# Weight loads on ScalarE's DMA queue, and attention slots moved to the first feed-forward half

## The chip, the core and the metric

The kernel runs on one core of a Trainium2 chip. A core has a matrix engine (TensorE, PE in the profile; its weight loads are PEld), a vector engine (VectorE, DVE), a scalar engine (ScalarE, ACT), a general engine (GpSimd, POOL) and a sync engine (SyncE, SP) that here only issues DMAs. Each engine works through its own list of instructions in order. DMAs are issued by SP and by ACT, each on a queue of its own (q1 and q10 in the profile); a DMA instruction that waits for something holds up whatever stands behind it on the engine that issues it. The metric is the device time of one execution in microseconds; less is better.

## The reference

```python
batch, n_heads, seq, head_dim = (8, 8, 576, 64)
n_tokens, d_model, d_ff = (4608, 512, 2048)

def _attn_ref(q, k, v, s):
    scores = scale * np.matmul(q, k.transpose(0, 1, 3, 2))
    cum = np.cumsum(np.maximum(s, 0.0), axis=-1)
    bias = -(cum[:, :, :, None] - cum[:, :, None, :])
    scores = np.where(causal, -1000000000.0, scores + np.minimum(bias, 0.0))
    scores = scores - np.max(scores, axis=-1, keepdims=True)
    attn = np.exp(scores)
    attn = attn / (np.sum(attn, axis=-1, keepdims=True) + 1e-09)
    return np.matmul(attn, v)

def _moe_ref(x, w_in, w_out):
    h = x @ w_in
    g = np.where(h >= 1, h, np.where(h <= -1, 0.0, (h + 1) ** 2 / 4))
    return g @ w_out
```

The output of the attention, with its heads side by side, is the input `x` of the feed-forward layer. The two weight matrices arrive as 64-bit numbers.

## The kernel before

**Attention.** Heads are taken in pairs, 32 pairs `n` for 8 batches of 4. A batch's 576 query rows are cut in two halves `hf`, of 320 and 256 columns. One pair in one half is a job: 64 jobs, for each batch four of the first half and then four of the second. A job is cut into 8 slots (`att_slot(j, k)`): slot 0 prepares Q and K, slots 2 to 7 each compute one block of scores, slot 3 also loads the next job's Q and K, and slot 7 also issues `att_out` of the job before. For a block of scores PE multiplies Q by K into a PSUM tile `s` (L405 for the first eight jobs, L410 and L411 later; there are two such tiles, shared with `px`), DVE adds the mask and finds the minimum `mn` (L416), ACT takes the exponential (L427), DVE gets the reciprocal of the sum `rs` (L443, L444), POOL, ACT and DVE write the scaled weights as two half-precision parts `pb` (L448 to L451, L454), and SP issues a DMA transpose of `pb` into `pt` (L455). `att_out` multiplies `pt` with `vt`, the transposed V, into `px` (L473), and ACT and DVE write it to `X[b, hf]` (L484 for the first half of all, L490 and L491 later). Names such as `p3_4_1` are pair 3, query tile 4, head 1.

**Weights.** Each matrix comes in 16 chunks of 512 KB (`Weights`, `w1` for `w_in`, `w2` for `w_out`). `load` (L190) brings a chunk into a raw buffer `wir` or `wor`; `decode` makes 32-bit floats of it: ACT L199, DVE L200, a matmul of the sums for a bound (L204), and then either ACT L212 and DVE L213 or DVE L215 and L216. The last of these frees the raw buffer for a later chunk. `w1` has four raw buffers; `w2` has two of one kind and two that it shares with tiles of `X`. `scale` takes the bound of a group of chunks (L220 to L223), and `split` makes two half-precision parts, with ACT L229 and L231 and POOL L232. The chunk's place in `WT` gives the name: `WT2` to `WT17` are the chunks of `w1` and `WT18` to `WT33` those of `w2` as they are decoded. The first three loads of `w2` wait for the bound of the last group of `w1`, by a small copy (L185).

**Feed-forward.** Its 16 halves run one after the other. The first half of all uses 32-bit matmuls (`first_h`, L566, needs `X[0, 0]` of the first four jobs and the decoded `w1`; `first_y`, L584, needs the decoded `w2`). All later halves use the split parts: `ffn_h` (L534) takes 16 tiles `h` one after the other, ACT, DVE and POOL make `g` of each, and `ffn_y` (L611) adds it into four tiles `y`, two steps behind.

**Order.** The program is written as loops: first four jobs with the 16 chunks of `w1`, then 512 steps `j`. In each step stand one attention slot, or two, then parts of the weights' work, then feed-forward work; step 32 opens the second half. A scheduler then sets the order of each engine's instructions: the written order is their priority, some parts have a higher one (`tc.high_priority`), and an instruction is taken when the scheduler believes that it can run. The order on the engines so differs from the written one.

Of the kernel before, what the change touches and what calls it, by code (L numbers as in the profile page):

```python
# [25 lines left out]
NFT = DFF // P  # L26
# [43 lines left out]
@with_exitstack  # L70
def attention_ffn(ctx: ExitStack, tc: tile.TileContext, qT, kT, vT, s, w_in, w_out, yT):
    nc = tc.nc
    LOADQ, CUMQ = nc.sync, nc.scalar
    V, A, G, T = nc.vector, nc.scalar, nc.gpsimd, nc.tensor

    cp = ctx.enter_context(tc.tile_pool(name="cp", bufs=1))
# [91 lines left out]
    class Weights:  # L168
# [10 lines left out]
        def load(self, n, after=None):  # L179
            if n < NW:  # L180
                c = self.order[n]
                pool, tag, bufs = self.tags[n % len(self.tags)]
                self.raw[c] = pool.tile([P, NC, 2], I32, tag=tag, bufs=bufs, name=f"{self.name}r{c}")
                if after is not None:
                    V.tensor_copy(self.raw[c][:, 0, :1], after.bitcast(I32))  # L185
                src = self.src(c)
                dst = self.raw[c]
                if len(src.shape) == 4:
                    dst = dst.rearrange("p (j n) t -> p j n t", j=2)
                nc.sync.dma_start(dst, src)  # L190

        def decode(self, n):
            c, g = self.order[n], n // self.size
# [79 lines left out]
    def batch_scales(b):  # L273
        m = msc[b]
        h = hsc[b] = ap.tile([P, 4], F32, tag="hs", name=f"hs{b}")
        V.tensor_scalar(h, w1.bound, m, 2.0 ** -27, ALU.mult, ALU.mult)

        r = rsc[b] = ap.tile([P, 1], F32, tag="r", name=f"r{b}")
        i = r.bitcast(I32)
        V.tensor_scalar(r, m, a_in, 4.0, ALU.mult, ALU.mult)  # L280
        V.tensor_scalar(r, r, 1.0, None, ALU.max)
        V.reciprocal(r, r)
        V.tensor_scalar(r, r, 2.0 ** 14, None, ALU.mult)
        V.tensor_scalar(i, i, 23, None, ALU.logical_shift_right)
        V.tensor_scalar(i, i, 127, None, ALU.add)
        V.tensor_scalar(i, i, 1, 23, ALU.logical_shift_right, ALU.logical_shift_left)

        u = usc[b] = ap.tile([P, 4], F32, tag="us", name=f"us{b}")
        V.tensor_scalar(u, h, r, None, ALU.mult)
        w = wsc[b] = ap.tile([P, 4], F32, tag="ws", name=f"ws{b}")  # L290
        V.tensor_scalar(w, u, 2.0, None, ALU.mult)
        c = ubi[b] = ap.tile([P, 1], F32, tag="ub", name=f"ub{b}")
        V.tensor_scalar(c, r, 0.5, None, ALU.mult)
        g = gsc[b] = ap.tile([P, 1], F32, tag="gb", name=f"gb{b}")
        V.reciprocal(g, r)
        V.tensor_scalar(g, g, g, 2.0 ** 14, ALU.mult, ALU.mult)

    def batch_y(b, groups=(0, 1)):
        ysc.setdefault(b, {})
        for i in groups:  # L300
            y = ysc[b][i] = ap.tile([P, 1], F32, tag=f"ys{i}", name=f"ys{b}_{i}")
            V.tensor_scalar(y, gsc[b], w2.bound[:, i:i + 1], 2.0 ** -28, ALU.mult, ALU.mult)
# [197 lines left out]
    def att_slot(j, k):  # L500

        if j < len(jobs):
            n, hf = jobs[j]
            if k == 0:
                att_prep(n, hf)
            if k == 1 and hf == 0:
                v_prep(n)
            if k == V_K and hf == 0:
                v_turn(n)
            if k >= 2:  # L510
                scores(n, *UNITS[hf][k - 2])
            if k == 3 and j + 1 < len(jobs):
                att_load(*jobs[j + 1])
            if k == 1 and j % (2 * NPAIR) == V_J and j // (2 * NPAIR) + 1 < B:
                load_v(j // (2 * NPAIR) + 1)
            if k == 5 and j + 1 < len(jobs) and jobs[j + 1][0] % NPAIR == 0 and jobs[j + 1][1] == 0:
                with tc.issue_after(ttr[0]):
                    batch_start(jobs[j + 1][0] // NPAIR)
        if k == OUT_K and 1 <= j <= len(jobs) and j != NPAIR:
            while j == len(jobs) and late:  # L520
                late.pop(0)()
            att_out(*jobs[j - 1])
# [39 lines left out]
    def first_h(ft):  # L562
        N = HALF[0][1]
        h = ps_h.tile([P, 512], F32, tag="h", name=f"h0_0_{ft}")
        for kt in range(NKT):
            T.matmul(  # L566
                h[:, :N], flat32(w1.held[ft // 4 * NKT + kt])[:, ft % 4 * P:(ft % 4 + 1) * P], X[0, 0][:, kt],
                start=(kt == 0), stop=(kt == NKT - 1),
            )
        if ft % 4 == 0:  # L570
            g32.append(gp.tile([P, 4, N], F32, tag="g", bufs=G_BUFS, name=f"g0_0_{ft}"))
        with tc.high_priority(offset=FFN_LEAD):
            u = gp.tile([P, N], F32, tag="u", bufs=4, name=f"u0_0_{ft}")
            A.activation(u, h[:, :N], AF.Relu, bias=half_bias, scale=us32)
            V.scalar_tensor_tensor(h[:, :N], h[:, :N], ws32, u, ALU.mult, ALU.max)
            V.scalar_tensor_tensor(g32[-1][:, ft % 4], u, 1.0, h[:, :N], ALU.min, ALU.mult)

    def first_y(ft, ms):
        N = HALF[0][1]
        for m in ms:  # L580
            if ft == 0:
                ys[0, 0, m] = ps_y.tile([P, 512], F32, tag=f"y{m}", name=f"y0_0_{m}")
            c0 = ft % 2 * 2 * P + m % 2 * P
            T.matmul(  # L584
                ys[0, 0, m][:, :N], flat32(w2.held[8 * (m // 2) + ft // 2])[:, c0:c0 + P], g32[ft // 4][:, ft % 4],
                start=(ft == 0), stop=(ft == NFT - 1),
            )
            if ft == NFT - 1:
                o = gp.tile([P, N], F32, tag="o", bufs=O_BUFS, name=f"o0_0_{m}")
                with tc.high_priority(offset=FFN_LEAD):  # L590
                    A.copy(o, ys[0, 0, m][:, :N])
                nc.scalar.dma_start(yT[m * P:(m + 1) * P, :N], o)
# [37 lines left out]
    def ffn_step(s, k):  # L630

        b, hf, ft = s // (2 * NFT), s // NFT % 2, s % NFT
        if k == 0:
            ffn_q.append((b, hf, ft, ffn_h(b, hf, ft)))
        elif len(ffn_q) > Y_LAG:
            ffn_y(*ffn_q.pop(0))
# [26 lines left out]
    for j in range(16 * NP):  # L663
        if j % 64 == 48 and j // 64 + 1 < B:
            batch_scales(j // 64 + 1)
            batch_y(j // 64 + 1)

        for _ in range(1 + (j % 4 == 3 if j < 2 * NFT else j % 8 == 3 and j < 6 * NFT)):
            att_slot(t // 8, t % 8)
            t += 1  # L670
        if j < NW // 2:
            with tc.high_priority(offset=W2_LEAD):
                for c in (2 * j, 2 * j + 1):
                    w2.decode(c)
                    w2.load(c + 3)
                    if c % 8 == 7:
                        w2.scale(c // 8, TINY)
        if j < NFT:
            first_h(j)
        elif j < 2 * NFT:  # L680
            i = j - NFT
            if i < 8:
                for ft in (2 * i, 2 * i + 1):
                    first_y(ft, (0, 1))
            else:
                for ft in range(i % 4 * 4, i % 4 * 4 + 4):
                    first_y(ft, (i // 4,))
        if j == NFT:
            V.tensor_reduce(a_in, w1.bound, axis=AX, op=ALU.max)
            batch_scales(0)  # L690
            batch_y(0)
        if 4 <= j < NW + 4:
            w1.split(j - 4)
        if NW + 8 <= j < 2 * NW:
            w2.split(j - NW - 8)
        elif 2 * NW <= j < 2 * NW + 4:
            with tc.high_priority(offset=W2_LEAD):
                for c in (8, 9):
                    w2.split(c + (j - 2 * NW) * 2)
        if j >= 2 * NFT:  # L700
            ffn_step(j // 2, j % 2)
# [32 lines left out]
```

## Time and profile before

| | |
|---|---|
| median of 3 runs | 1121.34 us (1119.88 to 1121.64) |
| the profiled execution | 1119.59 us, of which the span is 1117.8 |
| busy in the span | PE 1024.0 us, DVE 836.8, ACT 731.0, POOL 667.6 |
| granted TensorE clock, mean | 0.98 |
| DMA queues | q1 (SP) 143.49 MB, 60.3% of 16 engines' time; q10 (ACT) 9.93 MB, 2.9% |
| weight loads | 32 of 512 KB, issued from 1.4 to 142.6 us |

In a row of a timeline stand the start in us, the duration, the engine and the line, the operation with its output and input, how often it is repeated, and in brackets the idle time ahead of it and what ended that. "SPq" and "ACTq" are DMA issues; the transfer itself ends later. In a row of stretches the columns are named where it is shown. In the groups of the page stand the summed busy time, the mean of one in ns, and the idle time ahead.

### The profile page before, as it was taken

To read this page: it belongs to the slowest core of one execution; us is meant where nothing else is said; L and a number is where in the kernel's file an instruction comes from. 1 tells how busy PE (TensorE), PEld (TensorE's weight loads), DVE (VectorE), ACT (ScalarE), POOL (GpSimd) and SP (SyncE) were. 2 spreads that over 40 slices of the span, in tenths; PEclk is the share of its full clock that TensorE was granted. 3 is DMA by queue.
4 is the path that set the end of the run, shared out by engine and by line. 5 is a ranking of instruction groups with operands and counts; after the bars stand their busy time and mean duration, and the time that the engine had idled before them with its cause. 6 is when DMAs were issued, how large, how long until landed. Compare 5 with 4: busy or idle time off the path is not lost.

```text
span 1117.8 us, 24800 instructions
## 1 busy us (share of the span) xinstructions
PE 1024.0 (92%) x8366; PEld 787.3 (70%) x8368; DVE 836.8 (75%) x2313; ACT 731.0 (65%) x1703; POOL 667.6 (60%) x1163
## 2 busy tenths in 40 slices
PE   2668897699999999999999999899999999899998
PEld 1335565487777877777778877777778877787787
DVE  7865775778778877878778878777787877887533
ACT  4656669667557774767557774767577765777432
POOL 4642558776557654766557755666557664765522
PEclk9999899699998999999999999999999999999999
DMA  7995633687548763878658763878468763776300
GB/s 237 242 215 144 171 85 90 128 163 157 121 96 186 164 147 75 179 142 174 110 107 184 160 141 77 178 159 165 88 134 188 156 136 78 162 157 140 67 25 19
DMA packets 340774, 154.99 MB, mean 139 GB/s; under 512 B 290856, under 2 KB 322472, under 8 KB 340648
## 3 DMA queue, kind: packets, MB, share of 16 engines
q1 hardware_dynamic: 330944, 143.49, 60.3%
q10 hardware_dynamic: 9704, 9.93, 2.9%
q8 instruction: 66, 1.08, 0.4%
q14 instruction: 60, 0.49, 0.1%
HBM read 72.31 MB, written 9.73 MB: 73 GB/s over the span
## 4 chain that ended last, share of the span: by engine, by line
PE 55%; DVE 14%; POOL 9%; DMA 8%; ACT 7%; issue 6%; ACTq 0%; SPq 0%; DVEq 0%; POOLq 0%
PE h L534 23%; PE y L611 22%; PE px L473 3%; DMA pt<-pb 3%; PE s L410 3%; DVE pb L454 3%; PE s L411 3%; DMA wor<-in_moe_w_out_dram 2%; POOL pb L448 2%; POOL pb L451 2%; DVE p L416 2%; ACT p L427 2%; ACT u L546 2%; DVE Q L355 1%; DVE h L549 1%
## 5 line engine op out<-in xcount | busy, mean ns | idle before, releaser
L611 PE MATMUL y<-g,WT 128*128 128x256 f16 (+1 forms) x2880 | 427.5, 287 | 8.9 <-POOL g L599 6.9
L534 PE MATMUL h<-x,WT 128*128 128x256 f16 (+1 forms) x2880 | 428.6, 287 | 2.8 <-DVE x L491 2.1
L611 PEld LDWEIGHTS <-WT 128*128 128x128 f16 x2880 | 269.1, 98 | 84.1 <-issue 13.9
L534 PEld LDWEIGHTS <-WT 128*128 128x128 f16 x2880 | 270.6, 98 | 78.4 <-issue 6.0
L427 ACT ACTIVATE p<-p,mn 64x64 f32<-64x64 f32 (+4 forms) x320 | 179.2, 560 | 143.2 <-DVE mn L416 121.7
L599 POOL TENSOR_TENSOR g<-u,g 128x256 f16<-128x256 f32 (+1 forms) x240 | 189.6, 790 | 134.0 <-ACT g L598 133.1
L448 POOL TENSOR_SCALAR pb<-p,rs 64x128 f16<-64x128 f32 (+4 forms) x160 | 97.5, 610 | 213.6 <-DVE rs L444 140.7
L546 ACT ACTIVATE u<-h,ub,us 128x256 f32<-128x256 f32 (+1 forms) x240 | 139.4, 581 | 123.7 <-PE h L534 114.9
L549 DVE SCALAR_TENSOR_TENSOR h<-h,ws,u 128x256 f32<-128x256 f32 (+1 forms) x240 | 123.8, 516 | 102.3 <-ACT u L546 99.8
L451 POOL TENSOR_TENSOR pb<-p,pb 64x128 f16<-64x128 f32 (+4 forms) x160 | 172.8, 1080 | 9.5
L454 DVE SCALAR_TENSOR_TENSOR pb<-p,rs,pb 64x128 f16<-64x128 f32 (+4 forms) x160 | 139.0, 869 | 48.0 <-POOL pb L448 47.9
L416 DVE CUSTOM_DVE_ANT_0 p<-s,mask 64x64 f32<-64x64 f32 (+4 forms) x320 | 134.8, 421 | 32.7 <-PE s L411 22.0
L410 PE MATMUL s<-K,Q 128*64 128x64 f32 (+1 forms) x336 | 126.9, 379 | 17.4 <-DVE mn L416 10.3
L550 DVE SCALAR_TENSOR_TENSOR u<-u,r,h 128x256 f32<-128x256 f32 (+1 forms) x240 | 121.8, 507 | 6.6 <-DVE h L549 0.5
L449 ACT ACTIVATE p<-p,rs 64x64 f32<-64x64 f32 (+4 forms) x160 | 89.6, 560 | 55.4 <-DVE rs L444 53.7
L411 PE MATMUL s<-K,Q 68*64 68x64 f32 (+1 forms) x336 | 103.8, 310 | 4.4 <-DMA K<-cumd 3.2
L598 ACT CAST g<-u 128x256 f16<-128x256 f32 (+1 forms) x240 | 100.7, 419 | 5.9 <-DVE u L550 5.9
L450 POOL TENSOR_SCALAR pb<-p 64x128 f16<-64x128 f32 (+4 forms) x160 | 91.4, 571 | 15.2 <-ACT p L449 14.0
L473 PEld LDWEIGHTS <-vt 128*64 128x64 f16 x1536 | 72.8, 114 | 37.7 <-issue 21.5
L473 PE MATMUL px<-pt,vt 128*64 128x256 f16 (+3 forms) x1536 | 83.6, 260 | 10.7 <-DMA pt<-pb 7.8
L410 PEld LDWEIGHTS s<-K,Q 128*64 128x64 f32 (+1 forms) x336 | 62.1, 185 | 28.6 <-DVE mn L416 9.6
L411 PEld LDWEIGHTS s<-K,Q 68*64 68x64 f32 (+1 forms) x336 | 62.7, 187 | 7.7 <-ACT x L490 3.1
(115 smaller groups left out, 1139.3 us busy)
## 6 DMA issues: line engine op xcount, KB each, us to landing
rk<-in_k_dram SPq DMA_DIRECT2D x56, 288.0 KB
v<-in_v_dram SPq DMA_DIRECT2D x32, 288.0 KB
rq<-in_q_dram SPq DMA_DIRECT2D x56, 160.0 KB
rk<-in_k_dram SPq DMA_DIRECT2D x56, 160.0 KB
wir<-in_moe_w_in_dram SPq DMA_DIRECT2D x16, 512.0 KB
wor<-in_moe_w_out_dram SPq DMA_DIRECT2D x16, 512.0 KB
rq<-in_q_dram SPq DMA_DIRECT2D x56, 128.0 KB
out_dram<-o ACTq DMA_DIRECT2D x32, 160.0 KB
```

Of the source, the lines that this page charges most:

```text
L410: T.matmul(sc[:R, :c1 - c0], Q1[:, hd, qo:qo + R], K1[:, hd, c0:c1], start=True, stop=False)
L411: T.matmul(sc[:R, :c1 - c0], Q2[:KC, hd, qo:qo + R], K2[:KC, hd, c0:c1], start=False, stop=True)
L416: ttr[0] = V.tensor_tensor_reduce(out=Pt[:R, c0:c1], in0=sc[:R, :c1 - c0], in1=mask[:R, mo:mo + c1 - c0], scale=-0.125 if j < F32_JOBS els ...
L427: A.activation(Pt[:R, :W], Pt[:R, :W], AF.Exp, bias=m2[:R], scale=-1.0, accum_out=sums[n, i][:R, hd:hd + 1])
L451: G.tensor_tensor(los[1], pw, his[1], ALU.subtract)
L454: V.scalar_tensor_tensor(los[0], pv, rs[:R, :1], his[0], ALU.mult, ALU.subtract)
L473: T.matmul(px[hd * D:(hd + 1) * D, lo:N], VT[:, vl * NB + j, hd * D:(hd + 1) * D], PT[:, 4 * j + 2 * hd + pl, lo:], start=(m == 0), stop=( ...
L534: T.matmul(h[:, :N], w1.out[ft // 4 * NKT + kt][:, wl, ft % 4 * P:(ft % 4 + 1) * P], x[:, kt, xl], start=(n == 0), stop=(n == 3 * NKT - 1),)
L546: first = A.activation(u, h[:, :N], AF.Relu, bias=ubi[b], scale=usc[b][:, fg:fg + 1]).ins
L549: V.scalar_tensor_tensor(h[:, :N], h[:, :N], wsc[b][:, fg:fg + 1], u, ALU.mult, ALU.max)
L599: G.tensor_tensor(g[:, 1], u, g[:, 0], ALU.subtract)
L611: T.matmul(ys[b, hf, m][:, :N], w2.out[8 * (m // 2) + ft // 2][:, wl, c0:c0 + P], g[:, gl], start=(ft == 0 and n == 0), stop=(ft == NFT - ...
```

## The change

Two things change. All weight chunks' loads are issued by ACT and go on its queue; nothing is left on SP but `s`, Q, K, V, the running sums and the transposes, and two outputs at the end. And the second slot of a step comes in every second step of the first 32 (16 more slots there, where there were 8), and in no later step (before, in every eighth step from 32 to 95, 8 slots). The number of slots is the same in all, and from step 96 on each step has the same slots as before.

```diff
-    LOADQ, CUMQ = nc.sync, nc.scalar
+    LOADQ, CUMQ, WQ = nc.sync, nc.scalar, nc.scalar
...
-                nc.sync.dma_start(dst, src)
+                WQ.dma_start(dst, src)
...
-        for _ in range(1 + (j % 4 == 3 if j < 2 * NFT else j % 8 == 3 and j < 6 * NFT)):
+        for _ in range(1 + (j % 2 if j < 2 * NFT else 0)):
             att_slot(t // 8, t % 8)
             t += 1
```

The order shifts on every engine in the first two feed-forward halves. Three places:

The loads of the last two chunks of `w1` (`wir11` for `WT16`, `wir15` for `WT17`), before, on SP, among the transposes of the first and second pair:

```order
L455 DMA_TRANSPOSE pt0_0_222<-pb0_2_316 128x12x128
L455 DMA_TRANSPOSE pt1_0_361<-pb1_0_362 128x4x64
L319 DMA QF1_97<-in_q_dram 64x2x320
L319 DMA KF1_98<-in_k_dram 64x2x320
L381 DMA_TRANSPOSE vt2_533<-vb2_474 128x10x128
L455 DMA_TRANSPOSE pt1_0_361<-pb1_1_400 128x8x128
L190 DMA wir11_555<-in_moe_w_in_dram 128x1024
L455 DMA_TRANSPOSE pt1_0_361<-pb1_2_437 128x12x128
L190 DMA wir15_613<-in_moe_w_in_dram 128x1024
```

Now, on ACT, around the end of the second pair's exponentials:

```order
L427 ACTIVATE p1_2_0_421,sm1_2_420<-p1_2_0_421,mn1_2_0_0_425 128x320
L328 DMA KF1_98<-cumd_112 2x2x320
L190 DMA wir7_521<-in_moe_w_in_dram 128x1024
L449 ACTIVATE p1_1_1_393<-p1_1_1_393,rs1_1_401 128x192
L427 ACTIVATE p1_2_1_430,sm1_2_420<-p1_2_1_430,mn1_2_1_0_434 128x320
L199 ACTIVATE WT13_127<-wir14_472 128x512
L190 DMA wir11_555<-in_moe_w_in_dram 128x1024
L199 ACTIVATE WT14_128<-wir3_484 128x512
L449 ACTIVATE p1_2_1_430<-p1_2_1_430,rs1_2_438 128x320
L212 ACTIVATE wir3_484<-wir3_484,floor_bias_75 128x512
L199 ACTIVATE WT15_129<-wir7_521 128x512
```

The load of `wir11` has moved from behind four transposes of `pb` and `vt` on SP to ACT's list, where it stands right behind the second pair's last exponential and the step L199 of `wir14`, and ahead of all exponentials of the third pair.

DVE at the last `pb` of the fourth pair, the last step of it that DVE does, before:

```order
L444 RECIPROCAL rs3_2_715<-rs3_2_715 128x2
L289 TENSOR_SCALAR us0_1299<-hs0_1289,r0_1291 128x4
L293 TENSOR_SCALAR ub0_1303<-r0_1291 128x1
L295 RECIPROCAL gb0_1305<-r0_1291 128x1
L291 TENSOR_SCALAR ws0_1301<-us0_1299 128x4
L296 TENSOR_SCALAR gb0_1305<-gb0_1305 128x1
L454 SCALAR_TENSOR_TENSOR pb3_2_714<-p3_2_0_698,rs3_2_715,pb3_2_714 128x3x128
L200 TENSOR_SCALAR WT18_132<-WT18_132 128x512
L200 TENSOR_SCALAR WT19_133<-WT19_133 128x512
```

Now:

```order
L416 ISA mn3_2_1_0_711 128x1
L454 SCALAR_TENSOR_TENSOR pb3_1_679<-p3_1_0_661,rs3_1_680,pb3_1_679 128x2x128
L443 TENSOR_SCALAR rs3_2_715<-sm3_2_697 128x2
L444 RECIPROCAL rs3_2_715<-rs3_2_715 128x2
L200 TENSOR_SCALAR WT21_135<-WT21_135 128x512
L200 TENSOR_SCALAR WT22_136<-WT22_136 128x512
L454 SCALAR_TENSOR_TENSOR pb3_2_714<-p3_2_0_698,rs3_2_715,pb3_2_714 128x3x128
L200 TENSOR_SCALAR WT23_137<-WT23_137 128x512
L215 SCALAR_TENSOR_TENSOR WT21_135<-wor3_781,WT21_135 128x512
```

L454 of `pb3_2` stood ahead of the first chunk of `w2` (`WT18`); now the first decode steps of the fourth and fifth chunks (`WT21`, `WT22`) stand ahead of it, and those of the first three still further ahead.

ACT at the last exponential of the first batch (`p3_4_1`), whose result opens the second feed-forward half, before:

```order
L229 ACTIVATE WT26_140<-WT28_142,r_wo_153 128x512
L592 DMA out_0_dram<-o0_0_3_1733 128x320
L231 ACTIVATE WT28_142<-WT28_142,r_wo_153 128x512
L229 ACTIVATE WT27_141<-WT29_143,r_wo_153 128x512
L231 ACTIVATE WT29_143<-WT29_143,r_wo_153 128x512
L350 ACTIVATE Q1_1554<-rq4_0_1427 128x640
L229 ACTIVATE WT28_142<-WT30_144,r_wo_153 128x512
L353 CAST K1_1555<-rk4_0_1428 128x2x320
L427 ACTIVATE p3_4_1_1487,sm3_4_1437<-p3_4_1_1487,mn3_4_1_288_1503 128x576
```

Now:

```order
L231 ACTIVATE WT25_139<-WT25_139,r_wo_153 128x512
L229 ACTIVATE WT24_138<-WT26_140,r_wo_153 128x512
L231 ACTIVATE WT26_140<-WT26_140,r_wo_153 128x512
L350 ACTIVATE Q1_1521<-rq4_0_1405 128x640
L353 CAST K1_1522<-rk4_0_1406 128x2x320
L229 ACTIVATE WT25_139<-WT27_141,r_wo_153 128x512
L427 ACTIVATE p3_4_1_1465,sm3_4_1418<-p3_4_1_1465,mn3_4_1_288_1477 128x576
L229 ACTIVATE WT26_140<-WT28_142,r_wo_153 128x512
L490 ACTIVATE x0_1_1167<-px2_1_1488,ex0_307 128x256
```

The exponential stood behind the splits up to L231 of `WT29` and L229 of `WT30`; now it stands behind those up to L231 of `WT26` and L229 of `WT27`, and the splits of the last chunks follow it, six instructions more than before.

## The prediction

> **What bounds the kernel now.** I read the page first, then the busy table by stretches, then the waits and the timelines of the first 237 us.
>
> ```profile
> span 1117.8 us, 24800 instructions
> ...
> PE 1024.0 (92%) x8366; PEld 787.3 (70%) x8368; DVE 836.8 (75%) x2313; ACT 731.0 (65%) x1703; POOL 667.6 (60%) x1163
> ...
> PE   2668897699999999999999999899999999899998
> ```
>
> TensorE (PE) is busy 92% of the span, and its idle time stands almost wholly in the first nine of 40 slices. The stretches give its size:
>
> ```profile
> 0.00:86.00 86.00, 43.92 (x154) 22.80 (x155) 62.53 (x191) 44.70 (x96) 46.19 (x96) 0.98 0.90 234
> 86.00:120.00 34.00, 28.01 (x84) 17.08 (x85) 23.98 (x61) 22.02 (x39) 12.10 (x15) 0.85 0.51 130
> 120.00:185.00 65.00, 64.59 (x289) 43.64 (x289) 41.23 (x93) 51.97 (x91) 41.56 (x47) 1.00 0.51 119
> 185.00:237.00 52.00, 35.01 (x294) 27.66 (x293) 38.83 (x114) 36.20 (x90) 41.08 (x69) 0.77 0.59 125
> 237.00:1118.00 881.00, 852.49 (x7552) 676.13 (x7549) 670.22 (x1856) 576.08 (x1391) 526.67 (x939) 1.00 0.63 132
> ```
>
> The columns are PE, PEld, DVE, ACT and POOL busy, PE clock, DMA share, GB/s. PE idles 42.1 us before 86, 6.0 from 86 to 120, 0.4 to 185, 17.0 to 237 and 28.5 in the 881 us left. In both programs PE has the same matmuls, and from the ninth tile of the second half (about 237 us) its rows stand in the same order: at the start of every later half the same attention unit stands next to the same `h` tile. So the slot counts alone are costed at nothing; what hides them is that attention already runs as early as its own steps let it; were that cover gone, one job would move from beside the later matmuls to beside the earlier ones, with no work added. The time can only change before 237 us.
>
> **The change, part by part.** *The last first-layer weights.* ScalarE (ACT) now issues the 32 weight loads; SyncE (SP) keeps Q, K, V and the transposes. SP issued the loads of the last two `w_in` chunks late:
>
> ```profile
> 43.39 4.93 SPq L455 DMA_TRANSPOSE pt<-pb  x2
> 52.78 0.53 SPq L190 DMA_DIRECT2D wir<-in_moe_w_in_dram  x1
> 54.16 2.22 SPq L455 DMA_TRANSPOSE pt<-pb  x1
> 56.48 0.60 SPq L190 DMA_DIRECT2D wir<-in_moe_w_in_dram  x1
> ...
> 41.82 0.78 DVE L213 SCALAR_TENSOR_TENSOR WT<-wir,WT 128x512 int32<-128x512 int32 x1 [1.00 <-ACT p L449]
> 47.77 0.68 DVE L216 SCALAR_TENSOR_TENSOR WT<-wir,WT 128x512 int32<-128x512 int32 x1
> ...
> 68.44 0.68 DVE L220 TENSOR_REDUCE bound_wi<-sum_wi 128x1 f32<-128x512 f32 x1
> 72.53 0.26 DVE L185 COPY wor<-bound_wi 128x1 int32<-128x1 int32 x3
> ...
> L454 DVE SCALAR_TENSOR_TENSOR pb<-p,rs,pb 64x128 f16<-64x128 f32 (+4 forms) x160 | 139.0, 869 | 48.0 <-POOL pb L448 47.9
> L416 DVE CUSTOM_DVE_ANT_0 p<-s,mask 64x64 f32<-64x64 f32 (+4 forms) x320 | 134.8, 421 | 32.7 <-PE s L411 22.0
> ```
>
> Their buffers (four in turn) came free with the decodes that end at 42.6 and 48.45, so the loads at 52.78 and 56.48 were 10.2 and 8.0 us late, behind transposes that waited for VectorE. On ACT they stand ahead of the third job's exponentials. The last chunk then comes up to 8.0 us sooner; next in line is DVE, which in the new order has four minima (L416, 0.42) and two pb steps (L454, 0.87) fewer ahead of L220, 3.4 us. Between that and 8.0 I take 6: the second layer's loads, which L185 releases, start at 66.7 instead of 72.7.
>
> *What then ends the first four jobs.* PE is full from the moment px of the fourth job runs:
>
> ```profile
> 72.70 1.43 SPq L190 DMA_DIRECT2D wor<-in_moe_w_out_dram  x3
> 75.74 0.92 DVE L454 SCALAR_TENSOR_TENSOR pb<-p,rs,pb 128x384 f16<-128x384 f32 x1
> 77.45 3.34 SPq L455 DMA_TRANSPOSE pt<-pb  x1
> 77.59 0.43 DVE L200 TENSOR_SCALAR WT<-WT 128x512 int32<-128x512 int32 x1 [0.94 <-ACT WT L199]
> 84.08 1.65 PE L473 MATMUL px<-pt,vt 128*64 128x320 f16 x18 [2.18 <-DMA pt<-pb]
> 87.52 0.67 ACT L199 ACTIVATE WT<-wor 128x512 f32<-128x512 f32 x1 [0.87 <-DMA wor<-in_moe_w_out_dram]
> ...
> 199.38 3.60 SPq L455 DMA_TRANSPOSE pt<-pb  x1
> 205.35 2.77 PE L473 MATMUL px<-pt,vt 128*64 128x256 f16 x30 [5.39 <-DMA pt<-pb]
> ```
>
> Here the change adds a wait. L454 of that job stood ahead of every `w_out` chunk on DVE; now the first step (L200) of the fourth and fifth chunks stands ahead of it. The fifth chunk issued was ready 14.8 us after the first was issued (87.52 less 72.70). So px comes at 66.7 + 14.8 + 0.67 (L199) + 0.43 (L200) + 0.92 (L454) + the transposes. Those took 6.6 us (77.45 to 84.08) with three weight chunks issued ahead of them on the same queue; a job of 20 blocks took 6.0 us at 199 without, so 12 blocks by share 3.6. I take 4.6, since weights still run beside them. Sum 88.1 against 84.08: **a loss of 4.0**. Bounds: a loss of 2.0 with the loads at 64.7, a gain of 2 if the chunks also arrive faster than in that row, a loss of 12 if the loads don't start earlier and the transposes take 6.6.
>
> *The hole at 110.* At px the new order has `w_out` four to five chunks further on. Before, a late chunk cost PE this:
>
> ```profile
> 103.86 0.67 ACT L199 ACTIVATE WT<-wor 128x512 f32<-128x512 f32 x1 [1.73 <-DMA wor<-in_moe_w_out_dram]
> 105.04 2.57 ACT L212 ACTIVATE wor<-wor,floor_bias 128x512 uint16<-128x512 uint8 x2
> 108.83 0.17 DVE L443 TENSOR_SCALAR rs<-sm 128x2 f32<-128x2 f32 x1 [3.45 <-ACT p L427]
> 109.64 0.99 DVE L213 SCALAR_TENSOR_TENSOR WT<-wor,WT 128x512 int32<-128x512 int32 x1
> 115.16 1.33 PE L405 MATMUL s<-KF,QF 68*128 68x288 f32 x2 [4.63 <-DVE mn L416]
> ...
> 110.00:115.00 5.00, 0.53 (x2) 0.07 (x1) 5.00 (x6) 4.11 (x8) 4.92 (x5) 0.82 0.33 107
> 115.00:120.00 5.00, 4.84 (x9) 2.90 (x10) 4.82 (x18) 0.90 (x3) 1.22 (x4) 0.50 0.43 122
> ```
>
> ACT decodes two chunks back to back, the exponential waits behind them, DVE then decodes, and the score matmul waits 4.63 us for DVE's minimum. After it PE ran five us at half clock, 2.4 us of work lost. Idle of 86 to 120 is 6.0, so at most 8.4 comes back, and nothing if the chunks that are left make another such hole. I take **a gain of 6.0**.
>
> The Trainium skill, "TensorE: Matmul & The Clock Gate", Part 1, says that an idle window of about 3.4 us puts the array at half clock until it has been busy as long; the granted 0.50 behind the 4.5 us idle agrees. By that rule a hole that closes whole returns its half-clock time too, and the gain would be 8.4, the sum 2.4 us lower.
>
> *The hole at 187.* ACT ran the splits of `w_out` ahead of the last exponential of the first batch:
>
> ```profile
> 187.16 0.52 DVE L416 CUSTOM_DVE_ANT_0 p<-s,mask,mn 128x288 f32<-128x288 f32 x1
> 189.89 0.77 ACT L427 ACTIVATE p<-p,mn 128x576 f32<-128x576 f32 x1
> ```
>
> Its minimum was there at 187.7, so it stood 2.2 us behind others. The new order has six splits (0.72 us each, a row below) fewer ahead of it. The chain from there over the transposes to px at 205.35 opens the next half: **a gain of 2.2**, rounded to 2. It is at most 4.3, and a loss of 2 if the splits now behind it hold up the later steps.
>
> *ACT's time.* An issue is hidden where an instruction runs:
>
> ```profile
> 174.43 0.72 ACT L229 ACTIVATE WT<-WT,r_wo 128x512 f16<-128x512 f32 x1
> 174.56 0.41 ACTq L592 DMA_DIRECT2D out_dram<-o  x1
> ...
> 12.20 0.33 SPq L190 DMA_DIRECT2D wir<-in_moe_w_in_dram  x1
> 15.72 0.57 ACTq L324 DMA_DIRECT2D QF<-ch  x1
> 22.69 0.65 ACT L199 ACTIVATE WT<-wir 128x512 f32<-128x512 f32 x1
> ```
>
> The output's DMA lies within the 0.72 us ahead of it, so 32 loads of some 0.5 us (1.43 for three) cost nothing unless the queue waits. Queued behind a waiting load are ACT's exponentials, for which DVE, POOL and the score matmuls wait. One place is early: the fifth chunk's load now stands behind L324's, so it goes out at 16.3 instead of 12.2, and the sixth behind the fifth's L199, which puts its own L199 near 25.6 instead of 22.69; the later chunks, freed from SP, make this up by the ninth. Taken at 0, at worst a loss of 3.
>
> **The sum.** +4.0 - 6.0 - 2.0 + 0 = -4.0. The profiled execution took 1119.59 (span 1117.8 and 1.8 around it); that gives 1115.6. The median of the three runs, 1121.34, lies 1.75 above it, so 1117.3.
>
> **Rivals.** *Slower: ACT as a queue.* If the `w_out` loads don't start sooner (a load that waits for its buffer stops the exponentials, and these stop DVE's decode), px waits for the fifth chunk all the same: 72.7 + 14.8 + 2.0 + 4.6 = 94.1, a loss of 10; with half the hole at 110 gone and nothing at 187 the sum is +7, so **1128**. It decides from a start of the loads at about 70.7, where the loss at px eats the gains. For it: L427 waits on ACT's order already, and 32 more waits join it. Against: the order puts each load only a step or two behind the instruction that frees its buffer.
>
> *No change.* The loads' start and px move by as much as the hole at 110 returns, or another hole opens in its place: within 2.2 of **1121**. The measure can't tell less than 0.2% (2.2 us), as the runs spread over 1.8. For it: PE has 0.4 us of idle in 120 to 185, so a gain before must survive as an earlier end of that full stretch. The Trainium skill, "DMA: Bandwidth & Descriptors", "Issuing engines are not separate DMA queues", speaks against the change: several issuing engines save only sequencer time. Here that is 32 loads of about 0.5 us on SP, hidden, and by it the time stays 1121; the 10.2 us by which a load went out late are a wait in line, which the rule does not count.
>
> *Better.* Loads at 64.7 and faster transposes, so that px loses nothing, the whole 8.4, and 2 to 4 at 187: about -11, **1110**.
>
> **Chances.** The sum's case (1113 to 1120) 0.45, of which 0.03 lies within 0.2%; the better case 0.13; no change 0.16; slower 0.26. Faster 0.55, same 0.19, slower 0.26. The likeliest is 1117.3; its own range is 1113 to 1120. With the bounds of the terms and the slower case inside, the range is 1107 to 1129.
>
> **What would show it.** Right: weight loads on ACT's queue, L185 near 67, px of the fourth job between 86 and 90 with its DVE step waiting for a chunk's L200, no PE gap of 4 us between px and the end of the first feed-forward half's matmuls, the half clock there gone, and the end of the full stretch a few us before 185. Wrong: L185 at 72 or later; ACT idle behind L190 waits while PE waits for minima; px beyond 92; a new gap of 4 us or more in 90 to 180; or more than 2 us of difference behind 237, where the order is the same.

## The result and the profile after

The changed kernel is slower: 1128.32 us median (1124.57 to 1135.18) against 1120.87 (1119.67 to 1122.82) for the kernel before, ratio 1.0072 with a 95% interval of 1.0049 to 1.0096, 7.5 us more by the medians. Its profiled execution took 1124.57 us, 5.0 more than that of before. It is the quickest of the changed kernel's runs, so its trace shows about two thirds of the loss.

The table by stretches of the changed kernel has the same columns as before (PE, PEld, DVE, ACT and POOL busy, PE clock, DMA share, GB/s):

```profile
0.00:86.00 86.00, 41.87 (x137) 21.19 (x138) 64.18 (x193) 47.10 (x98) 47.59 (x94) 0.86 0.91 234
86.00:120.00 34.00, 28.42 (x103) 17.65 (x102) 22.71 (x54) 20.37 (x36) 9.83 (x15) 0.85 0.60 155
120.00:185.00 65.00, 61.40 (x267) 42.19 (x267) 38.45 (x93) 43.86 (x78) 36.88 (x43) 0.97 0.42 95
185.00:237.00 52.00, 36.18 (x279) 28.91 (x278) 40.69 (x114) 40.59 (x96) 44.67 (x71) 0.74 0.55 122
237.00:1122.70 885.70, 855.07 (x7586) 677.50 (x7584) 673.98 (x1862) 579.49 (x1399) 529.97 (x945) 1.00 0.63 132
```

PE's idle time up to 185 us is 53.3 us (44.1, 5.6 and 3.6 in the three rows) where it was 48.5. These 4.8 us are nearly the whole difference of the two profiled executions. From 185 to 237 us PE then idles 1.2 us less than before, and behind 237 us 2.1 us more (30.6 for 28.5).

The timeline of the changed kernel around px of the fourth job, rows of DVE, ACT and PE:

```profile
65.64 0.26 DVE L185 COPY wor<-bound_wi 128x1 int32<-128x1 int32 x3
65.81 0.43 ACTq L190 DMA_DIRECT2D wor<-in_moe_w_out_dram  x1
83.41 0.66 ACT L199 ACTIVATE WT<-wor 128x512 f32<-128x512 f32 x1 [0.20 <-DMA wor<-in_moe_w_out_dram]
85.02 0.85 DVE L454 SCALAR_TENSOR_TENSOR pb<-p,rs,pb 128x384 f16<-128x384 f32 x1 [0.48 <-POOL pb L448]
90.52 2.30 ACTq L190 DMA_DIRECT2D wor<-in_moe_w_out_dram  x3
90.57 1.65 PE L473 MATMUL px<-pt,vt 128*64 128x320 f16 x18 [0.69 <-DMA pt<-pb]
94.48 0.66 ACT L199 ACTIVATE WT<-wor 128x512 f32<-128x512 f32 x1 [5.70 <-DMA wor<-in_moe_w_out_dram]
95.04 0.52 ACT L484 ACTIVATE x<-px,ex 128x320 f32<-128x320 f32 x1
95.61 2.50 PE L566 MATMUL h<-x,WT 128*128 128x320 f32 x4 [1.60 <-ACT x L484]
```

The loads of `w_out` start 6.9 us sooner than before (65.81 for 72.70), yet px of the fourth job comes 6.5 us later (90.57 for 84.08) and its x write 8.9 us later (95.04 for 86.13). Between px and the x write ACT ran nothing: three load issues (90.52), which waited for buffers, stood ahead of it, and behind them the first step of a chunk, which waited for one of those loads to land. The x write comes 4.47 us after px's start; in the kernel before 2.05, by this row of it:

```profile
86.13 0.52 ACT L484 ACTIVATE x<-px,ex 128x320 f32<-128x320 f32 x1
```

Further on, stretches of the kernel before and then of the changed one, same columns:

```profile
100.00:120.00 20.00, 14.07 (x40) 7.97 (x39) 13.19 (x33) 12.88 (x22) 8.59 (x12) 0.83 0.57 126
120.00:160.00 40.00, 39.59 (x178) 26.32 (x180) 28.41 (x64) 28.39 (x50) 20.50 (x23) 1.00 0.62 146
```

```profile
60.00:80.00 20.00, 11.71 (x41) 6.32 (x39) 15.87 (x62) 10.29 (x26) 8.70 (x22) 0.54 0.87 232
80.00:100.00 20.00, 13.23 (x54) 7.44 (x55) 9.48 (x21) 10.56 (x19) 4.24 (x10) 0.60 0.75 180
...
100.00:120.00 20.00, 20.00 (x75) 13.20 (x72) 16.86 (x43) 14.46 (x27) 8.99 (x12) 1.00 0.55 149
120.00:160.00 40.00, 36.40 (x152) 24.57 (x152) 25.88 (x64) 27.05 (x47) 22.49 (x26) 0.96 0.46 102
```

The hole at 110 is gone: PE is busy all of 100 to 120, 5.9 us more than before. But 3.2 us are lost again from 120 to 160, and the clock column reads about half (0.54, 0.60) through 60 to 100. That column has to be held against the matmuls' own times. The first layer's matmuls (L566) from 60 to 80 us and from 90 to 100, before:

```profile
L566 PE MATMUL h<-x,WT 128*128 128x320 f32 x8 | 4.8, 761 | 1.2 <-ACT x L484 1.2
...
L566 PE MATMUL h<-x,WT 128*128 128x320 f32 x19 | 5.6, 432 | 0.1
```

and in the changed kernel:

```profile
L566 PE MATMUL h<-x,WT 128*128 128x320 f32 x4 | 2.5, 781 | 0.0
...
L566 PE MATMUL h<-x,WT 128*128 128x320 f32 x4 | 2.5, 781 | 1.6 <-ACT x L484 1.6
```

From 60 to 80 one takes 761 ns before, where the column says 1.00, and 781 in the changed kernel, where it says 0.54: they are equally slow. The difference comes later. From 90 to 100 the kernel before has reached 432 ns, and the changed one, with its PE still waiting for the x write, has not.

The opening of the second half, PE, DVE and ACT rows of the changed kernel:

```profile
188.48 0.27 PE L104 MATMUL row_m<-ident,mt 128*1 128x128 f32 x1
191.28 0.52 DVE L416 CUSTOM_DVE_ANT_0 p<-s,mask,mn 128x288 f32<-128x288 f32 x1
195.25 0.76 ACT L427 ACTIVATE p<-p,mn 128x576 f32<-128x576 f32 x1
209.66 2.77 PE L473 MATMUL px<-pt,vt 128*64 128x256 f16 x30 [4.32 <-DMA pt<-pb]
```

In the kernel before, the first of these stood here, and the last at 205.35:

```profile
184.64 0.27 PE L104 MATMUL row_m<-ident,mt 128*1 128x128 f32 x1
```

So the changed kernel enters the second half 3.8 us late and leaves its opening 4.3 us late; nothing was won there.

### The profile page after: what moved, and what is told of

Its sections match the earlier page's. It is cut to its first block, busy times and chain, and to the rows that moved or that the text cites. A ratio compares the mean times of both kernels' runs of the same rounds, so it can differ in the third digit from the quotient of the medians.

```text
span 1122.7 us, 24779 instructions
## 1 busy us (share of the span) xinstructions
PE 1022.9 (91%) x8368; PEld 787.4 (70%) x8368; DVE 840.0 (75%) x2313; ACT 731.4 (65%) x1703; POOL 668.9 (60%) x1163
## 4 chain that ended last, share of the span: by engine, by line
PE 51%; DVE 13%; POOL 6%; issue 5%; DMA 5%; ACT 4%; ACTq 0%; DVEq 0%; POOLq 0%; SPq 0%
PE h L534 22%; PE y L611 21%; DMA pt<-pb 4%; PE px L473 3%; PE s L410 3%; DVE pb L454 3%; PE s L411 3%; DVE Q L355 2%; ACT u L546 2%; POOL pb L448 2%; DVE p L416 2%; DVE h L549 1%; DVE u L550 1%; ACT p L427 1%; DVE K L358 1%
## 5 line engine op out<-in xcount | busy, mean ns | idle before, releaser
L454 DVE SCALAR_TENSOR_TENSOR pb<-p,rs,pb 64x128 f16<-64x128 f32 (+4 forms) x160 | 141.6, 885 | 43.5 <-POOL pb L448 43.3
```

The source lines that it names most:

```text
L454: V.scalar_tensor_tensor(los[0], pv, rs[:R, :1], his[0], ALU.mult, ALU.subtract)
```

## The experiments

All have the new slots unless said otherwise. "slots_only" is the changed kernel with the loads left on SP; most others are edits of it. Ratios are to the kernel before, measured beside each kernel, with 95% intervals; its median differed a little from one set of runs to the next, so ratios are what to compare.

| label | what | median, us | ratio |
|---|---|---|---|
| (the change) | 32 loads on ACT | 1128.32 | 1.0072 (1.0049 to 1.0096) |
| wq_only | the same, old slots | 1131.54 | 1.0091 (1.0070 to 1.0112) |
| slots_only | loads on SP | 1119.33 | 0.9977 (0.9959 to 0.9995) |
| w1act | only `w_in` on ACT | 1131.48 | 1.0086 (1.0067 to 1.0104) |
| w2act | only `w_out` on ACT | 1125.72 | 1.0042 (1.0026 to 1.0058) |
| w1half | last 8 of `w_in` on ACT | 1125.39 | 1.0027 (1.0014 to 1.0040) |
| w1late | last 2 of `w_in` on ACT | 1121.56 | 0.9993 (0.9976 to 1.0010) |
| poolq | 32 loads on POOL's queue | 1130.25 | 1.0072 (1.0050 to 1.0094) |
| sphi | loads on SP, planned first | 1119.02 | 0.9971 (0.9958 to 0.9985) |
| sphi_old | the same, old slots | 1118.61 | 0.9976 (0.9960 to 0.9992) |
| lag | as the change, loads a chunk later | 1136.11 | 1.0128 (1.0099 to 1.0156) |
| touch_act | 32 small copies on ACT | 1122.68 | 1.0002 (0.9986 to 1.0017) |
| hold_act | these copies wait for the buffer | 1125.70 | 1.0031 (1.0014 to 1.0049) |
| dum_sync | 12 reads more, on SP | 1124.56 | 1.0024 (1.0004 to 1.0044) |
| dum_scalar | the same reads on ACT | 1132.45 | 1.0094 (1.0067 to 1.0121) |

### Loads or slots, first layer or second

The code cuts here and below are shortened; each shows what a kernel has in place of the kernel before (or, for "lag", of the changed one).

```diff
 slots_only   +for _ in range(1 + (j % 2 if j < 2 * NFT else 0)):
 wq_only      +WQ = nc.scalar;  WQ.dma_start(dst, src)
 w1act        +(nc.scalar if self.name == 'wi' else nc.sync).dma_start(dst, src)
 w2act        +(nc.scalar if self.name == 'wo' else nc.sync).dma_start(dst, src)
```

> All 32 weight loads on ACT, second slots as in the kernel before. Up to px of the fourth job the order is that of the changed kernel, word for word. Theory Q2 (second-layer loads that wait for a buffer hold ACT, and the fourth x write stands behind them): px of the fourth job near 90.6, its x write near 95, time 1127 to 1130. Theory O1 (the first-layer loads on ACT make the planned order place six instead of three second-layer chunks ahead of that px): the same here, 1127 to 1130. Theory S (the slots): 1121, and px near 84 to 86.

> All loads on SP as before, second slots as in the changed kernel; the order up to the fourth x write is that of the kernel before. Theories Q2 and O1: 1119 to 1123, with px of the fourth job at 84. Theory S (16 attention slots beside the first feed-forward half delay its matmuls): 1126 to 1129, with the loss between 90 and 237 us.

> First-layer loads on ACT, second-layer loads on SP, new slots. Theory O1: the order still has six second-layer chunks ahead of px of the fourth job on PE, so px at 88 to 92 and 1125 to 1130. Theory Q2: no second-layer load holds ACT any more, so the x write follows px by 2 us or less and the time is 1119 to 1122. Theory S: 1128.

> First-layer loads on SP, second-layer loads on ACT, new slots. Theory Q2: ACT waits 2 us or more behind a second-layer load ahead of the fourth x write, and the time is 1126 to 1130. Theory O1: three chunks ahead of px as before, px at 84 to 86, time 1119 to 1123. Theory S: 1128.

The slots are not the cause: alone they bring a little (0.9977), and the loads alone lose it all (1.0091). Both layers' loads cost on ACT, and the first layer's alone cost as much as all. That was not expected by the theory of the x write behind second-layer loads, which gave w1act 1119 to 1122. In w1act px of the fourth job came at 95.28, with six `w_out` chunks ahead of it on PE, so the order theory (O1, and O below) was still alive. The next four tell these apart.

### How many loads, which queue, which order

```diff
 w1late       +(nc.scalar if self.name == 'wi' and n >= 14 else nc.sync).dma_start(dst, src)
 w1half       +(nc.scalar if self.name == 'wi' and n >= 8 else nc.sync).dma_start(dst, src)
 poolq        +nc.gpsimd.dma_start(dst, src)
 sphi         +with tc.high_priority(offset=4000):
 sphi         +    nc.sync.dma_start(dst, src)
```

> slots_only (new slots, loads on SP: 1119.3) with only the last two first-layer loads on ACT. Theory M (loads and transposes on two queues run side by side and slow each other): two loads beside the transposes, px of the first four jobs 0 to 2 us later, time 1118 to 1122. Theory O (what costs is how many second-layer chunks the order places ahead of px of the fourth job; here 3, as before): 1118 to 1121. Theory A (loads on ACT stand in line behind its compute work from the first chunks on): 1117 to 1120. If these two loads come as much earlier as their lateness on SP (10 and 8 us), L185 is near 67 and the time 1113 to 1117.

> slots_only with the last eight first-layer loads on ACT, the first eight on SP. Theory M: the loads from 30 us on meet the transposes, px of the first job at 50 to 55 and 1123 to 1130. Theory A: the first eight chunks are decoded as on SP, so px of the first job at 48 to 50 and 1118 to 1122. Theory O (4 chunks ahead of px of the fourth job): 1120 to 1124.

> slots_only with all weight loads issued by POOL, on a third queue; ACT issues none. 2 second-layer chunks ahead of px of the fourth job. Theory M: the loads still run beside the transposes, px of the first job at 51 to 56, time 1125 to 1132. Theory O: 1117 to 1121. Theory A: 1117 to 1121, with ACT's first decodes as in the kernel before. POOL's own work for the issues is not in any row so far; if it is what costs, POOL stands busy or idle behind the loads while ACT and DVE wait for it.

> slots_only with all loads on SP, but planned with a higher priority, so that they stand ahead of transposes on the same queue; the order then has 7 second-layer chunks ahead of px of the fourth job on PE (before 3, changed kernel 6). Theory O: that px at 88 to 92 and 1125 to 1130, as with the loads on ACT. Theory M: one queue, so px of the first three jobs as in slots_only within 2 us, and 1116 to 1123. Theory A: 1116 to 1121.

The loss grows with the number of first-layer loads taken off SP's queue: 0.9977 with none, 0.9993 with 2 (the intervals of these two overlap), 1.0027 with 8, 1.0086 with 16. Theory A falls with w1half, which it put at 1118 to 1122 and which took 1125.39. Taking the loads to POOL costs as much as taking them to ACT, but poolq doesn't tell why: POOL is busy with each issue (about 0.6 to 0.7 us, last section) and stood idle 21 us in all ahead of them. The order theory falls with sphi. Its rows (lines stand one further down; SP, PE and ACT):

```profile
59.14 1.42 SPq L191 DMA_DIRECT2D wor<-in_moe_w_out_dram  x3
90.36 1.08 PE L474 MATMUL px<-pt,vt 128*64 128x320 f16 x18 [2.21 <-DMA pt<-pb]
91.48 0.53 ACT L485 ACTIVATE x<-px,ex 128x320 f32<-128x320 f32 x1 [2.75 <-PE px L474]
```

Seven `w_out` chunks stand ahead of px of the fourth job there, and px comes at 90.36, as late as in the changed kernel. Yet sphi is faster than the kernel before. Its x write follows px at once (ACT was waiting for px, not for a load), and its `w_out` loads started at 59.14. So a late px is paid back when the chunks are further on, as the prediction had it; what the changed kernel pays for is something else.

Theory M's forecast for px of the first job shows in w1late: 54.77 for 50.29 in slots_only, more than the 2 us that were forecast. The two loads that differ go out right beside the last transposes of that job. Rows of w1late (ACT, SP, PE), then its DMA view from 50 to 55 us (packets, MB, share of 16 engines), then the rows of slots_only:

```profile
44.72 2.88 ACTq L190 DMA_DIRECT2D wir<-in_moe_w_in_dram  x1
45.48 4.90 SPq L455 DMA_TRANSPOSE pt<-pb  x2
54.77 1.65 PE L473 MATMUL px<-pt,vt 128*64 128x320 f16 x18 [4.27 <-DMA pt<-pb]
...
q10 hardware_dynamic: 219, 0.78, 85.2%
q1 hardware_dynamic: 347, 0.09, 8.8%
```

```profile
44.71 4.72 SPq L455 DMA_TRANSPOSE pt<-pb  x2
50.29 1.65 PE L473 MATMUL px<-pt,vt 128*64 128x320 f16 x18
```

In slots_only px starts 0.9 us after SP has issued the job's last transpose (44.71 + 4.72), in the kernel before at once, in sphi after 1.4 us. In w1late it is 4.4 us: the loads on ACT's queue (q10) take the DMA engines from 50 to 55, and SP's queue (q1) moves next to nothing. With all 16 first-layer loads on ACT the same distance is 7.8 us (w1act) and 8.7 (wq_only), with px waiting for its transposes in both. So weight loads on a second queue do delay transposes. What that costs is another matter: in w1late px of the fourth job is level again with slots_only (86.89 and 86.61), and the kernel's time is nearly the same. In the changed kernel's own profile the distance at the first job is 3.8 us, and its row shows no wait of PE.

### Waiting, and the second queue, each by itself

Two causes were left, and the runs so far allow both. H: a load that waits for its buffer holds the in-order engine that issues it (POOL as well as ACT). M: loads and transposes on two queues run side by side and delay each other.

```diff
 hold_act     +A.copy(self.raw[c][:, 0, :1].bitcast(F32), half_bias)
 hold_act      nc.sync.dma_start(dst, src)
 touch_act    +A.copy(tok, hw[:, :1].bitcast(F32))      # behind L199, waits for nothing new
 lag          +w1.load(c + 2)                           # was c + 3; w2 alike
 dum_scalar   +nc.scalar.dma_start(d, w_in[...])        # d in DRAM; dum_sync: nc.sync
```

> slots_only (1119.3, all loads on SP) where ACT, ahead of each load, writes one element of the raw buffer: ACT then waits for the buffer exactly where it would wait to issue the load, but the load goes on SP's queue. Theory H (a load that waits for its buffer holds an in-order compute engine, whichever issues it): the loss of the changed kernel comes back, 1125 to 1131, with ACT idle 2 us or more ahead of exponentials or x writes. Theory M (loads and transposes on two queues slow each other): 1118 to 1123.

> slots_only with 32 small copies on ACT as in hold_act, but each reads one element of a chunk right behind that chunk's first decode step, so it waits for nothing new. Theory H (the wait of ACT for a buffer costs): 1118 to 1121, well below hold_act's 1125.7. If 32 more ACT instructions of 0.19 us are what hold_act pays for: 1124 to 1127.

In hold_act, the group of these copies and what ended ACT's idle time ahead of them (us, times; its lines from 190 on stand one further down, so L214 is L213 of the kernel before):

```profile
L190 ACT COPY wir<-half_bias x16: 173/188/268, 2.0 to 59.4; 128x1 f32<-128x1 f32 x16
L190 ACT COPY wor<-half_bias x16: 174/190/192, 74.7 to 149.5; 128x1 f32<-128x1 f32 x16
...
its engine sat idle before it (us, times) until:
  DVE WT L214: 5.6, 6
  DVE c L259: 5.3, 1
  DVE WT L217: 3.5, 4
```

ACT stood still 14.4 us ahead of these copies, with every load on SP: 9.1 us until a decode step of DVE that frees a buffer (L214, L217), and once 5.3 us until another step of DVE. The kernel lost 0.54% to slots_only, at the low end of what H forecast. touch_act says that 0.25% of it is the 32 copies; the wait itself is the other 0.29%, some 3 us. The two intervals just overlap (to 1.0017 and from 1.0014), so H is probably there, but small.

> The changed kernel with all loads on ACT, each written one chunk later (after the decode of the chunk two ahead, not three), so that its buffer is mostly free when ACT reaches it. Theory H: ACT waits less, the x write of the fourth job follows its px within 2 us, time 1118 to 1124. Theory M: the two queues are still there, 1125 to 1131.

lag is worse than the change and than both forecasts, so a load that comes later does not help. It does not decide between the two, as each load is also a chunk later.

> slots_only with 12 more reads of 512 KB of a weight matrix into unused DRAM, issued by ACT between about 187 and 250 us, waiting for nothing. Theory M: the transposes beside them land later than with the same reads on SP; 2 to 6 us slower than dum_sync. Theory H: ACT is not held, so within 2 us of dum_sync. 12 reads are 6.3 MB; at the 135 GB/s of this stretch there is room for them.

> The same 12 reads issued by SP, each behind a transpose on its queue. Theory M: 1119 to 1123, each transpose at most 2 us later. Theory H: within 2 us of dum_scalar; both 1119 to 1125.

This pair speaks for M. No read waits for anything and nothing waits for a read, but on ACT's queue the 12 cost 0.7% more than on SP's, 7.9 us by the medians (2 to 6 were forecast), with intervals apart. The reads' place changes with the queue, though: on SP each stands behind a transpose and the first goes out at 201.37, on ACT the first goes out at 191.88. So the pair shows the price of reads that leave SP's order, not that of a second queue at equal places. The place where it shows first, dum_sync's PE row and then dum_scalar's issues (ACT, SP) and PE row:

```profile
203.21 2.77 PE L473 MATMUL px<-pt,vt 128*64 128x256 f16 x30 [4.07 <-DVE Q L355]
```

```profile
197.21 6.23 SPq L455 DMA_TRANSPOSE pt<-pb  x2
198.05 0.55 ACTq L505 DMA_DIRECT2D dum<-in_moe_w_in_dram  x1
202.73 0.52 ACTq L505 DMA_DIRECT2D dum<-in_moe_w_in_dram  x1
207.24 2.77 PE L473 MATMUL px<-pt,vt 128*64 128x256 f16 x30 [8.69 <-DMA pt<-pb]
```

The same px comes 4.0 us later, and now it is the transposes that it waits for. Up to it PE's order is the same in both; behind it the two differ in some places, so a part of the 7.9 us may be order, not of these 4.0. Nearly all of it falls while the reads run, up to 253 us: px of a later job, at 279.64 in dum_sync, comes 6.8 us later in dum_scalar (286.46), and from there on the lag stays within 6.5 to 8.5. The DMA view (packets, MB, share of 16 engines) of dum_scalar from 198 to 203 us and from 203 to 207, and of slots_only from 198 to 203:

```profile
q1 hardware_dynamic: 2211, 0.79, 114.0%
q10 hardware_dynamic: 11, 0.04, 2.5%
...
q10 hardware_dynamic: 207, 0.75, 81.2%
q1 hardware_dynamic: 763, 0.19, 28.9%
```

```profile
q1 hardware_dynamic: 3349, 1.11, 111.3%
```

In 198 to 203 SP's queue moved 2211 packets where it moves 3349 with no read beside it, at the same share of the engines: 41 ns a packet (80 us of 16 engines times 1.14, by 2211) for 27. The read issued at 198.05 has only 11 packets on record by 203. From 203 both queues run together, the reads with most of the engines, and the last transposes land at 207. The 41 ns by themselves are no sign of a second queue. The kernel before has the same, 43 ns, from 100 to 105, with one queue and its own loads among the transposes:

```profile
q1 hardware_dynamic: 2187, 0.90, 117.1%
```

The Trainium skill, "DMA: Bandwidth & Descriptors", "Issuing engines are not separate DMA queues", says that DMAs from several engines run on the same 16 DMA engines and interleave, and that a second issuing engine saves only sequencer time. That both queues' packets run on the same engines is what these rows show (q10 and q1 from 203 to 207); the 8 us that 12 reads cost more on ACT, their earlier place included, are more than the page's "only" lets one expect.

### The slots and the earlier loads

> sphi (all loads on SP, planned ahead of the transposes) with the second slots of the kernel before. If the slots' gain (0.9977) and the earlier loads' are separate: 1119 to 1123, and sphi keeps both. If the earlier loads do the same work as the slots: 1117 to 1121, as sphi. If the slots alone carry sphi's gain: 1121 to 1124.

sphi_old has sphi's edit and the old slot counts. It and slots_only gain as much as sphi does with both (0.9976, 0.9977, 0.9971; the intervals overlap widely), so no second gain on top of the first is seen. sphi, 1119.02 us, is faster than both kernels, by 0.3% and about 1%; it gives the weights their early place without a second queue.

## Why the prediction was wrong

- **Start of the `w_out` loads, 66.7:** right, 65.81. Their early place is worth having: sphi has it.
- **px of the fourth job, 88.1:** it came at 90.57, a loss of 6.5 for 4.0. The transposes took 4.70 us (85.87 to 90.57) as taken, 4.6. What was mis-sized is the fifth chunk, 17.6 us behind the first load (83.41 less 65.81) and not 14.8.
- **"PE is full from the moment px of the fourth job runs":** failed. The x write stood behind three loads that waited for buffers, and PE's next first-layer matmuls waited for it until 95.61.
- **The hole at 110, a gain of 6.0:** right in its place, 5.9. But 3.2 went again in new holes up to 160, and the quick L566 of before (432 ns from 90 to 100) came only after 100 (781 until then, 435 from 100 to 120).
- **The hole at 187, a gain of 2:** nothing. The exponential started 3.5 us behind its minimum (191.80 to 195.25) where it was 2.2, with ACT's splits still ahead of it.
- **The slots, costed at nothing:** nearly so; slots_only gains 0.23%.
- **ACT's time, costed at 0, at worst 3:** this is the step that failed. An issue does hide behind a running instruction (in the changed kernel one of 0.40 us at 78.24 lies within L212's 1.44 from 77.54). But moving the loads cost the change 0.95% to slots_only, 10.7 us. Two things are in it. ACT's waits for buffers, which the working named and bounded at 3, cost about 3 us (hold_act less touch_act), and in the changed kernel's profile they hold the fourth x write. The other, that ACT's queue and SP's transposes then share the DMA engines, has no term in the working; the profile of before has no row for it, since nearly all its bytes go on one queue. That it happens with weight loads is shown (in w1late, w1act and wq_only px waits for transposes until 4.4 to 8.7 us behind SP's last issue; in the kernel before, slots_only and sphi it comes within 1.4). Its price is not: the some 7 us that are left are a subtraction. The pair of reads gives a like size, with other transfers, at another place, and with their place moved too. The dose of loads and poolq fit both causes.
- **The slower rival, 1128:** its time was met, in part by luck. One half of its mechanism holds (a load that waits stops ACT), the other does not (the loads did start sooner, so px at 94.1 did not come).

## What to carry to other kernels

Before you move loads to a second queue, ask which short transfers run beside them. Here px of the first job came within 1.4 us of SP's last transpose in the three one-queue kernels compared; with weight loads on a second queue it waited up to 8.7 us, while the loads had a large share of the DMA engines. If a load goes out late, move it forward on its own queue first. And where a compute engine issues the load, look whether its buffer is free when the engine gets there; if not, whatever stands behind it waits too.

## What was not expected of the hardware

- Two queues do not share evenly from moment to moment. In w1late SP's queue had 8.8% of the engines from 50 to 55 us and ACT's loads 85.2%; in dum_scalar it was the other way round from 198 to 203 (SP's queue 114.0%, ACT's 2.5%), and it turned from 203 on (28.9% and 81.2%). What decides whose turn it is is open.
- The clock column can mislead in the first 100 us: in the kernel before it reads 1.00 from 60 to 80 us, where L566 took 761 ns, and 1.00 from 90 to 100, where it took 432.
- An issue by POOL lies on POOL itself, 0.53 to 0.79 us each, while ACT's lies beside its work:

```profile
23.20 0.58 POOL L190 DMA_DIRECT2D wir<-in_moe_w_in_dram  x1
```
